# Mixture-of-experts kernel on one core: the second expert weight loaded after the row transposes, and scaled and split in its own expert's first stage

## Chip, cores and metric

The kernel runs on one core of a Trainium2 chip. The metric is the device time of one execution in microseconds; lower is better. The engines are named as in the profile: PE (TensorE, the matrix engine) with its weight loads PEld, DVE (VectorE), ACT (ScalarE), POOL (GpSimd) and SP (SyncE, which here only issues DMAs).

## The reference

Attention with a banded mask in half of the heads and a strided mask in the other half, and behind it a layer of experts with a capacity. Only the second part matters here:

```python
def _moe_ref(x, w_gate, w1, w2):            # x: 4608 tokens x 512
    N, D = x.shape                          # w1: 8 x 512 x 1024, w2: 8 x 1024 x 512
    E = w_gate.shape[1]                     # 8 experts
    cap = N // E                            # 576 tokens for each
    logits = x @ w_gate
    # all (token, expert) pairs in order of falling logit: a token goes to the
    # first expert that is not full, until every token has one
    ...
    for e in range(E):
        mask = assigned == e
        h = np.maximum(x[mask] @ w1[e], 0.0)
        out[mask] = h @ w2[e]
```

Since every expert takes exactly 576 tokens, the greedy assignment can be done expert by expert: the expert that fills first is closed, its tokens leave, and so on.

## The kernel before, in words

The attention part writes the tokens' rows to a scratch tensor in DRAM (`x_scr`) and the logits to SBUF. It ends before 205 us of the profiled execution. Behind it the eight experts follow one after the other, in an order that the data decide; the number `ph` counts them from 0 to 7.

**What is done for one expert.** A search with seven rounds (`search`, L809 to L861) finds the logit at which the expert is full. Each round compares all logits with 17 candidates on DVE (`cm`, L817), counts on PE (L833), adds up on DVE (`red` L836, `r` L839) and PE (L842), compares on DVE (`g`, L846 or L849), sums on PE (L852) and makes the next candidates on DVE (`cand`, L855). From the result come the expert's number (`ei`, L877), each token's slot (`slots`, L886 to L916) and the list of its rows (`indices`, L935 to L974, with two groups of matmuls on PE, L961 and L969). POOL gathers the rows (`xr`, L1078: five gathers of up to 128 rows), ACT and DVE cut each row into two f16 parts (`xg`, L1067 and L1068), and SP issues a DMA transpose for each (`xt`, L1069). The last expert needs no search (`rest`, L864).

**The weights** (`weights`, L976 to L1052). SP reads the expert's number into a register and issues the loads (L985): four of 512 KB for w1 and four of 512 KB for w2. Each weight has one f32 buffer, so a load waits until the expert before has no more use of it. For each weight there are then: four squares with a sum on ACT (`jk`, L1000), a scale (`ss` on DVE L1006, a matmul with ones on PE L1008, four small steps on DVE L204 to L209, which end in `w_sw`), and eight cuts (L1018 and L1019) in which ACT makes the upper f16 half (`w1h`, `w2h`) and DVE the lower one (`w1l`, `w2l`). The f16 halves have two buffers.

**The two stages of an expert on PE** (`ffn`, L1185). First stage: 8 blocks of 24 matmuls (`hidden`, L1175), each followed by the ReLU on ACT (`hh`, L1182) and its lower half on DVE (`hl`, L1183). Second stage: four and a half tiles of 128 rows, 24 matmuls each (L1223, the half one L1217); ACT scales the result (`y`, L1233), and POOL scatters it to the output (L1234). Before the second stage stand two small DVE steps, L1205 and L1206, that multiply the two weights' scales.

**What sets the order.** Only PE's order is written by hand: `ffn` yields the cost of each matmul to a clock, and generators (`chains`) that hold the side work have due times on that clock in ns. When one is due, its next step is emitted there, so that the PE instructions of the search, the indices and the scales stand at that place between the matmuls. In the first expert ACT's order is held too (`MANP`). For all the other engines what is emitted first has the higher priority, and what stands in `urgent()` a higher one still; a planner orders them by that when the whole program is known, and each engine then works through its queue in order.

For `ph` 1 and later the chain of the weights is one list: a step of 4000 ns (`T_W`), four squares of w1 (1500 ns each), its scale (1500), then four pairs of a cut of w1 and a square of w2, two more cuts of w1, the scale of w2, two cuts of w1 and eight cuts of w2 (1500 each). It starts when the expert's number is known, which is about when the first stage of the expert before ends. What is left of it when the own first stage begins is emitted at once (`rush`, in `spread`). For `ph` 0 there is a separate path (`start`, `more`, `later`), which the change leaves as it is.

The gather and the transposes are a chain of their own (`fetch`): the indices, then the five conversions and transposes in steps of 5000 and then 1200 ns, then 3000 ns more until the expert counts as ready.

Of the kernel before, what the change touches and what calls it, by code (L numbers as in the profile page):

```python
# [57 lines left out]
SCALE_AT, TURN_AT, TAKE_AT, SEARCH_AT, TURN_U, W_EARLY, TURNS, TURN_E = 7, 9, 9, 10, 0, 1, 3, 2  # L58
T_HOT6, T_CLOSE6 = 3200, 9000
T_F, T_LOAD0, T_HOT1, T_W, T_SQ, T_SCALE, T_CUT, T_BULK0 = 3000, 1500, 6350, 4000, 1500, 1500, 1500, 600  # L60
CUT0 = 1
# [76 lines left out]
def band_stride_attention_then_capacity_moe(ctx, tc, qt, kl, ks, nl, ns, wg, w1, w2, cst, out, dbg=None):  # L138
# [82 lines left out]
    with tc.tile_pool(name="ld", bufs=2) as ld, \  # L221
# [317 lines left out]
        todo = [Unit(b, strided) for b in range(B) for strided in (True, False)]  # L539
# [200 lines left out]
    def spread(ph, todo):  # L740
        for step, f in todo:
            if ph not in rush:
                yield step if ph else min(step, T_BULK0)
            f()

    def slowly(todo):
        for step, f in todo:
            yield min(step, T_STEP0) if step != T_W20 else step
            f()
# [226 lines left out]
    def weights(ph, ei):  # L976
        e = nc.sync.value_load(ei[0:1, 0:1], min_val=0, max_val=E - 1)
        res, todo = [], []
        for name, w, nch, width, bits in (("w1", w1, DC, FF, W1_BITS), ("w2", w2, FC, DM, W2_BITS)):
# [6 lines left out]

            k = W_EARLY if ph == 0 and name == "w2" else 4
            fetch_w(range(k))
            if k < 4:
                def later(wf=wf, k=k, n4=n4, go=fetch_w):  # L990
                    nc.gpsimd.memset(wf[:, k * n4:, :1], 0.0)
                    go(range(k, 4))
# [34 lines left out]
        if ph == 0:  # L1027
# [17 lines left out]
            return res, (start, more, later)  # L1045
        todo = [(T_W, lambda: None)] + sq1 + sc1
        for a, b in zip(cut1[:4], sq2):
            todo += [a, b]
        todo += cut1[4:6] + sc2 + cut1[6:] + cut2
        g = spread(ph, todo)  # L1050
        chains.append([due_now(), g])
        return res, g  # L1052

# [102 lines left out]
    def fetch(ph, slot, wts):  # L1156
        idx, sx = yield from indices(ph, slot)
        xt, todo = tokens(ph, idx)
        for t, f in enumerate(todo):
            yield T_ROWS if t == 0 else T_ROW  # L1160
            f()
        yield T_LOAD - T_ROWS
        work[ph] = wts[0], xt, idx, sx, wts[1]
        ready.add(ph)
# [20 lines left out]
    def ffn(ph, wts, xt, idx, sx):  # L1185
# [14 lines left out]
        else:  # L1200
            for f in range(FC):
                yield from hidden(wts, xt, hh, hl, f, (slice(0, HC), slice(HC, CAP)), ps_h.tile([128, 2, 512], F32, name="ph"))
        for _ in second[0] if ph == 0 else ():
            pass
# [3 lines left out]
        for t in (0, NT - 1, *range(1, NT - 1)):  # L1208
            tail = t == NT - 1
            py = ps_h.tile([128, 2, 512], F32, name="ph")[:, 0]  # L1210
            k = 0
# [49 lines left out]
    with tc.manual_schedule(engines=MAN):  # L1261
        work[0] = now[:4] + (now[4](),)
        chains.append([T_LOAD0, load0()])
        for ph in range(E):
            with tc.manual_schedule(engines=MAN0) if ph in MANP else nullcontext():
# [5 lines left out]
                for c in list(chains):  # L1271
                    if c[1] is work[ph][4]:
                        c[0] = clock
                        advance(c)
                for cost in ffn(ph, *work[ph][:4]):
                    clock += cost
# [70 lines left out]
```

## Time and profile before

| | |
|---|---|
| median of three runs | 678.89 us (674.91 to 679.88) |
| the profiled execution's own time | 676.12 us |
| its span, first to last instruction | 674.4 us |
| mean granted PE clock | 0.959 |
| w loads: number, size | 64 of 512 KB |
| HBM read / written | 73.60 MB / 18.87 MB |
| first stage of `ph` 0 begins | 220.36 us |
| second stage of `ph` 7 begins | 639.38 us |

A line of the timeline has the start in us, the duration in us (of the whole group, where equal instructions in a row are merged), the engine, the line of the kernel, the operation, output <- inputs by the program's names, the shape and the count. In brackets behind it stands how long the engine was idle before, and what released it. A group line has the busy time and the mean in ns of one instruction, then the idle time before the group. A line of the waits has: who waited for whom, us in total, times, the longest. Groups that overlap in the merged timeline share their place: a merged line shows the first start, and other instructions of that engine may stand inside it.

### The profile page before, as it was taken

The numbers are of one execution on the slowest core, as the hardware profiler recorded it, in microseconds if no ns is written. First come the engines' busy times: TensorE is split into PE (matmuls) and PEld (weight loads), VectorE is DVE, ScalarE is ACT, GpSimd is POOL, SyncE is SP. The second block draws the span as 40 slices with busy tenths as digits, with TensorE's granted clock in tenths as the row PEclk, the third lists the DMA queues.
The fourth block names the chain that finished last, engine by engine and source line by source line (L and its number), as shares of the span: only waits on it lengthen the run. The fifth ranks groups of instructions, "written<-read, shape, count | busy, mean of one in ns | idle before, by whom it ended". The sixth has DMA issues, their size and how long they took to land.

```text
span 674.4 us, 19427 instructions
## 1 busy us (share of the span) xinstructions
PE 602.9 (89%) x8125; PEld 394.4 (58%) x8128; DVE 456.9 (68%) x1381; ACT 333.0 (49%) x554; POOL 110.8 (16%) x124
## 2 busy tenths in 40 slices
PE   7789899999847788999899989989989997999993
PEld 4567676776633564476467458447646744746741
DVE  4858787788787787777686786777768648570200
ACT  2555554555303464843851871664384279761210
POOL 2101101111102000500420430240042041211011
PEclk9959999999967799999999999989999999899997
DMA  8888798887406406803921860860491197911010
GB/s 240 200 231 222 209 241 239 246 234 215 137 2 216 129 1 236 209 17 131 268 63 35 299 129 1 286 160 17 174 245 44 67 306 228 240 35 48 1 40 32
DMA packets 76363, 102.40 MB, mean 152 GB/s; under 512 B 41292, under 2 KB 49062, under 8 KB 75763
## 3 DMA queue, kind: packets, MB, share of 16 engines
q1 hardware_dynamic: 68195, 79.61, 41.5%
q0 software_dynamic: 7360, 21.15, 10.4%
q8 instruction: 64, 1.05, 0.6%
q10 hardware_dynamic: 720, 0.39, 0.2%
q14 instruction: 24, 0.20, 0.1%
HBM read 73.60 MB, written 18.87 MB: 137 GB/s over the span
## 4 chain that ended last, share of the span: by engine, by line
PE 46%; issue 16%; DVE 15%; DMA 11%; ACT 6%; POOL 3%; SPq 1%; another core or an unknown queue 0%; POOLq 0%; ACTq 0%; DVEq 0%
PE ph L1175 17%; PE ph L1223 7%; PE po L394 4%; PE spa L351 4%; DMA w<-in_w_dram 4%; DMA xr<-x_scr,idx 2%; DVE w2l L1019 2%; DVE w1l L1019 2%; POOL xr L1078 2%; ACT jk L292 2%; DMA v_s<-in_ns_dram 2%; POOL out_dram L1234 1%; PE spb L469 1%; PE spa L374 1%; ACT w1h L1018 1%
## 5 line engine op out<-in xcount | busy, mean ns | idle before, releaser
L1175 PE MATMUL ph<-xt,w1h 128*128 128x288 f16 (+2 forms) x1024 | 177.9, 289 | 7.0 <-DMA xt<-xg 4.5
L1175 PEld LDWEIGHTS <-w1h 128*128 128x128 f16 x1024 | 97.7, 99 | 38.0 <-issue 8.5
L1175 PE MATMUL ph<-xt,w1l 128*128 128x288 f16 (+2 forms) x512 | 111.8, 289 | 0.0
L1234 POOL DMA_INDIRECT out_dram<-y,idx x40 | 47.8, 1195 | 337.2 <-ACT y L1233 314.6
L1223 PE MATMUL ph<-w2h,hh 128*128 128x512 f16 x256 | 97.8, 382 | 0.0
L1223 PE MATMUL ph<-w2h,hl 128*128 128x512 f16 x256 | 97.7, 382 | 0.0
L1223 PE MATMUL ph<-w2l,hh 128*128 128x512 f16 x256 | 97.5, 381 | 0.0
L1182 ACT ACTIVATE hh<-ph 128x576 f16<-128x576 f32 (+2 forms) x72 | 42.8, 595 | 108.6 <-PE ph L1175 108.0
L1000 ACT ACTIVATE jk<-w 128x1024 f16<-128x1024 f32 x64 | 67.4, 1053 | 57.8 <-DMA w<-in_w_dram 56.8
L1223 PEld LDWEIGHTS <-hh 128*128 128x128 f16 x512 | 49.4, 98 | 57.4 <-issue 7.2
L1183 DVE SCALAR_TENSOR_TENSOR hl<-ph,hh 128x576 f16<-128x576 f32 (+2 forms) x72 | 49.5, 687 | 43.7 <-ACT hh L1182 43.5
L1175 PEld LDWEIGHTS <-w1l 128*128 128x128 f16 x512 | 50.4, 99 | 13.3 <-issue 0.6
L1078 POOL DMA_INDIRECT xr<-x_scr,idx x40 | 41.6, 1040 | 51.2 <-DMA w<-in_w_dram 25.3
L377 ACT ACTIVATE pr<-spa 128x576 f32<-128x576 f32 x32 | 20.8, 651 | 57.6 <-PE spa L374 52.7
L1223 PEld LDWEIGHTS <-hl 128*128 128x128 f16 x256 | 25.1, 98 | 39.6 <-issue 14.8
L1019 DVE SCALAR_TENSOR_TENSOR w1l<-w,w_sw,w1h 128x512 f16<-128x512 f32 x64 | 45.6, 742 | 3.7 <-ACT w1h L1018 2.5
L1019 DVE SCALAR_TENSOR_TENSOR w2l<-w,w_sw,w2h 128x512 f16<-128x512 f32 x64 | 46.3, 744 | 2.1 <-ACT w2h L1018 2.0
L1018 ACT ACTIVATE w2h<-w,w_sw 128x512 f16<-128x512 f32 x64 | 41.1, 710 | 6.6 <-DVE w_sw L209 6.6
L1018 ACT ACTIVATE w1h<-w,w_sw 128x512 f16<-128x512 f32 x64 | 42.8, 709 | 3.0 <-DVE ss_e L204 1.8
L1233 ACT ACTIVATE y<-ph,so 128x512 f32<-128x512 f32 x32 | 21.8, 680 | 44.5 <-PE ph L1223 30.7
L428 POOL DMA_DIRECT2D x_scr<-xs x23 | 16.5, 724 | 154.0 <-DVE vsum L297 101.4
L394 PE MATMUL po<-v_s,pr 64*54 64x65 f32 x768 | 31.3, 230 | 2.4 <-DMA v_s<-in_ns_dram 1.5
(619 smaller groups left out, 920.3 us busy)
## 6 DMA issues: line engine op xcount, KB each, us to landing
w<-in_w_dram SPq DMA_DIRECT2D x64, 512.0 KB
kl<-in_kl_dram SPq DMA_DIRECT2D x16, 304.0 KB
v_s<-in_ns_dram SPq DMA_DIRECT2D x16, 292.5 KB
v_l<-in_nl_dram SPq DMA_DIRECT2D x16, 292.5 KB
ks<-in_ks_dram SPq DMA_DIRECT2D x16, 288.0 KB
qs<-in_qt_dram SPq DMA_DIRECT2D x16, 288.0 KB
ql<-in_qt_dram SPq DMA_DIRECT2D x16, 288.0 KB
x_scr<-xl SPq DMA_DIRECT2D x8, 512.0 KB
```

Of the source, the lines that this page charges most:

```text
L351: nc.tensor.matmul(u.sp[p][64 * f:64 * f + m, h, o:o + n], u.kt[r, p * u.nk + c:p * u.nk + c + m], u.q[r, p, c:c + n], start=False, stop=F ...
L394: nc.tensor.matmul(po[r:r + u.nq, j - j0], pr[k, o:o + u.nq], u.vn[k, t, 2 * p + h], start=(j == j0), stop=(j == j1 - 1), skip_group_check ...
L1000: nc.scalar.activation(jk, wf[:, c * n4:(c + 1) * n4].rearrange("p c f -> p (c f)"), AF.Square, scale=1.41422, accum_out=sq[:, c:c + 1])
L1018: nc.scalar.activation(hi[:, c, f], wf[:, c, f], AF.Copy, scale=s_)
L1019: nc.vector.scalar_tensor_tensor(lo[:, c, f], wf[:, c, f], s_, hi[:, c, f], op0=OP.mult, op1=OP.subtract)
L1078: nc.gpsimd.indirect_dma_start(out=xr[:n], out_offset=None, in_=x_rows, in_offset=bass.IndirectOffsetOnAxis(ap=idx[:n, t:t + 1], axis=0))
L1175: nc.tensor.matmul(tile_[:, j, :w], wt[:, d, f * 128:(f + 1) * 128], xt[:, d // 2, xx, d % 2, c], start=(k == 0), stop=(k == 3 * DC - 1))
L1182: nc.scalar.activation(hv, src, AF.Relu)
L1183: nc.vector.scalar_tensor_tensor(lv, src, 0.0, hv, op0=OP.max, op1=OP.subtract)
L1223: nc.tensor.matmul(py, a[:, f, ts_], w[:, f], start=(k == 0), stop=(k == len(todo) - 1))
L1233: nc.scalar.activation(y, py, AF.Copy, scale=so[:, t:t + 1])
L1234: st = nc.gpsimd.indirect_dma_start(out=out_rows, out_offset=bass.IndirectOffsetOnAxis(ap=idx[:n, t:t + 1], axis=0), in_=y[:n], in_offset= ...
```

## The change

For `ph` 1 and later: the four loads of w2 are no longer issued in `weights` but by a function (`later`) that `fetch` calls after the last row conversion and transpose have been emitted. The chain of the weights ends with the eight cuts of w1, now 1500 ns apart without squares between them. The squares, the scale and the cuts of w2 form a chain of their own (`thirds`), which starts when the expert's own first stage starts: a step of 4000 ns, four squares and the scale 1500 ns apart, then the eight cuts 1000 ns apart. What is left of it is emitted at the end of the first stage. `ph` 0 is as before.

```diff
+T_W21, T_CUT2 = 4000, 1000
...
+    thirds = {}
+
+    def evenly(todo):
+        for step, f in todo:
+            yield step
+            f()
+
...
-            k = W_EARLY if ph == 0 and name == "w2" else 4
+            k = 4 if name == "w1" else 0 if ph else W_EARLY
             fetch_w(range(k))
-            if k < 4:
+            if k == 0:
+                later = lambda go=fetch_w: go(range(4))
+            elif k < 4:
                 def later(wf=wf, k=k, n4=n4, go=fetch_w):
                     nc.gpsimd.memset(wf[:, k * n4:, :1], 0.0)
                     go(range(k, 4))
...
-        todo = [(T_W, lambda: None)] + sq1 + sc1
-        for a, b in zip(cut1[:4], sq2):
-            todo += [a, b]
-        todo += cut1[4:6] + sc2 + cut1[6:] + cut2
-        g = spread(ph, todo)
+        g = spread(ph, [(T_W, lambda: None)] + sq1 + sc1 + cut1)
         chains.append([due_now(), g])
-        return res, g
+        thirds[ph] = evenly([(T_W21, lambda: None)] + sq2 + sc2 + [(T_CUT2, f) for _, f in cut2])
+        return res, g, later
...
         for t, f in enumerate(todo):
             yield T_ROWS if t == 0 else T_ROW
             f()
+        wts[2]()
         yield T_LOAD - T_ROWS
...
-        for _ in second[0] if ph == 0 else ():
+        for _ in second[0] if ph == 0 else thirds[ph]:
             pass
...
+                if ph:
+                    chains.append([clock, thirds[ph]])
                 for cost in ffn(ph, *work[ph][:4]):
```

## The prediction, on record before the changed kernel was run

> **What bounds the kernel now.** I read the page first, then TensorE (PE) in order of time for the stage boundaries, then the list of PE's waits, then ACT, DVE and SP around those waits.
>
> ```profile
> span 674.4 us, 19427 instructions
> PE 602.9 (89%) x8125; PEld 394.4 (58%) x8128; DVE 456.9 (68%) x1381; ACT 333.0 (49%) x554; POOL 110.8 (16%) x124
> ```
>
> PE is busy for 89% of the span, so a change beside PE can win only what PE loses in waits or at a lower clock. In order of time, the first matmul of each stage marks its start: L1175 opens a first stage, L1223 a second one.
>
> ```profile
> 422.38 0.38 PE L1223 MATMUL ph<-w2h,hh 128*128 128x512 f16 x1
> 453.50 0.65 PE L1175 MATMUL ph<-xt,w1h 128*128 128x288 f16 x4
> 479.07 0.38 PE L1223 MATMUL ph<-w2h,hh 128*128 128x512 f16 x1
> 560.14 0.28 PE L1175 MATMUL ph<-xt,w1h 128*128 128x288 f16 x1
> 592.09 0.38 PE L1223 MATMUL ph<-w2h,hh 128*128 128x512 f16 x1
> 615.86 0.65 PE L1175 MATMUL ph<-xt,w1h 128*128 128x288 f16 x4
> 639.38 0.38 PE L1223 MATMUL ph<-w2h,hh 128*128 128x512 f16 x1
> ```
>
> Number the experts 0 to 7 in order of work. Expert 3's second stage takes 453.50 - 422.38 = 31.1 us, expert 4's first stage 25.6 us, expert 6's first stage 32.0 us, and expert 7's, with no search beside it, 23.5 us. The first stages of the middle experts are near that floor; the second stages and expert 6's first stage are not. The waits of PE between 285 and 615 us say where (in total, times, longest):
>
> ```profile
> PE ph L1175 <- DMA xt<-xg: 4.5, 2, 2.9
> PE pr__7371 L842 <- DVE red L836: 2.5, 1, 2.5
> PE pr__9134 L961 <- DVE rv L947: 1.9, 1, 1.9
> PE pr__6686 L842 <- DVE r L839: 1.6, 1, 1.6
> PE pr__8136 L852 <- DVE g L849: 1.3, 1, 1.3
> PE pr__5841 L842 <- issue: 1.1, 1, 1.1
> PE pr__5841 L852 <- DVE g L849: 1.0, 1, 1.0
> PE pr__5921 L842 <- DVE r L839: 0.9, 1, 0.9
> PE pr__8216 L842 <- DVE r L839: 0.9, 1, 0.9
> ...
> PE pr__7560 L842 <- DVE r L839: 0.3, 1, 0.3
> ```
>
> Two waits are for transposed rows (xt), before experts 1 (1.6) and 6 (2.9). One is for expert 7's index tables (rv), inside expert 6's first stage. The seven after that, 9.3 us together, are steps of the threshold search (L842, L852) in the second stages of experts 1 to 4: PE's order is written by hand, a search matmul stands in it at a fixed place, and all matmuls behind it wait when DVE is late. The last row is the same wait in a first stage, where it is small. Twice PE also runs at a lower granted clock soon after a wait:
>
> ```profile
> 445.00:450.00 5.00, 5.00 (x18) 1.97 (x17) 4.82 (x10) 3.65 (x6) 1.71 (x1) 0.66 1.06 237
> 455.00:465.00 10.00, 9.71 (x94) 7.58 (x92) 9.43 (x24) 6.76 (x11) 0.61 (x1) 1.00 0.08 29
> 465.00:475.00 10.00, 10.00 (x100) 8.13 (x98) 5.62 (x16) 1.95 (x3) 0.00 (x0) 1.00 0.01 2
> 575.00:580.00 5.00, 5.00 (x39) 3.12 (x32) 1.23 (x4) 3.55 (x7) 2.09 (x3) 0.66 0.80 279
> ```
>
> Columns: stretch, its length, then busy us of PE, weight loads, DVE, ACT, POOL, the clock, DMA share, GB/s. 5 us at 0.66 cost 5 x 0.34 = 1.7 us each time.
>
> **Part 1: the load.** The change emits the second weight's four DMAs after the last row transpose instead of at once. Only PE keeps the emitted order here; the other engines, SP among them, are ordered by a planner. Does that order follow what is emitted, or what is ready?
>
> ```profile
> 422.64 5.08 SPq L985 DMA_DIRECT2D w<-in_w_dram  x8
> 441.50 7.77 SPq L1069 DMA_TRANSPOSE xt<-xg  x5
> ...
> 455.07 0.16 DVE L1205 TENSOR_TENSOR s<-w_sw,w_sw 128x1 f32<-128x1 f32 x1
> 538.07 0.13 DVE L877 TENSOR_SCALAR ei<-wm 1x1 int32<-1x1 f32 x1
> ...
> 433.41 1.06 ACT L1000 ACTIVATE jk<-w 128x1024 f16<-128x1024 f32 x1
> 437.55 1.93 ACT L1018 ACTIVATE w1h<-w,w_sw 128x512 f16<-128x512 f32 x3
> ```
>
> It follows what is ready. L1205 is emitted behind all matmuls of the first stage, which ends at 479.07, yet runs at 455.07, as soon as both scales exist: 24 us early. Expert 7's number (538.07) is emitted only once expert 5 is done (560.14): 22 us early. A square of the second weight (433.41) runs ahead of the first weight's cut (437.55), which is emitted before it. So I expect SP to do the same: between 427.7 (the eighth load issued) and 441.50 (the first transpose) SP has nothing ready, the expert's number is in its register, and the buffer is free, since the last cut of the expert before ends by then (Part 3). The four loads then go out directly behind the first weight's four, as now: **0 us**. The transposes keep their place in SP's queue. Should the loads really move, the gather and the transposes are passed by 2 MB less; that is the first rival.
>
> **Part 2: the squares.** Four squares per expert (1.05 us each) are now emitted in the expert's own first stage. They too become ready when the chunk lands and still fill ACT's gaps in the second stage before; but now they give way to every cut of the first weight, where before they stood between them.
>
> ```profile
> L1000 ACT ACTIVATE jk<-w 128x1024 f16<-128x1024 f32 x64 | 67.4, 1053 | 57.8 <-DMA w<-in_w_dram 56.8
> L1019 DVE SCALAR_TENSOR_TENSOR w2l<-w,w_sw,w2h 128x512 f16<-128x512 f32 x64 | 46.3, 744 | 2.1 <-ACT w2h L1018 2.0
> L1018 ACT ACTIVATE w2h<-w,w_sw 128x512 f16<-128x512 f32 x64 | 41.1, 710 | 6.6 <-DVE w_sw L209 6.6
> ```
>
> ```profile
> 389.12 1.04 ACT L1000 ACTIVATE jk<-w 128x1024 f16<-128x1024 f32 x1
> 394.34 0.73 DVE L1019 SCALAR_TENSOR_TENSOR w1l<-w,w_sw,w1h 128x512 f16<-128x512 f32 x1
> 395.24 0.17 PE L842 MATMUL pr__6686<-r,fold 68*128 68x8 f16 x1 [1.60 <-DVE r L839]
> ```
>
> One square stands at 389.12 between cuts; the cuts behind it come 1.04 us later on ACT, their DVE halves too (the last at 394.34), and the search's sum queues behind that half, so PE waits 1.60 us. The three waits of this kind are 1.6, 0.9 and 0.9. Each can shrink by at most the square: 1.0 + 0.9 + 0.9 = 2.8. A part of each is the half itself (0.73), which stays, so I take **-2.0**; bounds -3.4 (all three gone) and +1.0 (a square that fills a gap just ahead of a row conversion, once). The waits of 2.5, 1.3, 1.1 and 1.0 stand earlier, among the row conversions, and I leave them. Expert 1's 1.6 for xt and expert 6's 2.9 each have one square ahead of a row conversion (expert 6's at 550.67, below): at most 1.04 each; a cut can take the freed place, so **-0.5** each, bounds 0 and -1.04.
>
> **Part 3: scale and cuts.** The scale's matmul (L1008) moves from the stage's boundary to 11.5 us into it (4 + 4 x 1.5 + 1.5 by the planner's steps), the eight cuts behind it. What they cost on DVE is the same 8 x 0.744 = 5.95 us; today they also run in the own first stage, but at its head: from 455 to 465 DVE is busy for 9.43 of 10 us, from 465 to 475 for 5.62. Moved to 12 us, they need 5.95 us out of DVE's remaining share (1 - 0.56 = 0.44 of the time): 13.5 us at worst, 9 us as they run now, so done 21 to 25.5 us into a stage of 25.6. The second stage needs the eighth half only some 4.6 us after its start (23.8 us in expert 6 for four and a half tiles of eight groups: 5.3 a tile, seven eighths of it), so it is covered; without that cover each missing half would cost 0.74. The search steps that the cuts pass cost PE 0.3 us at the head of the stage (pr__7560); I expect the same at its tail, where that wait also holds the number of the next expert, which SP's loads are waiting for: **+0.2** for each of four experts, +0.8; bounds -1.2 (the 0.3 gone four times, none new) and the second rival. In the last expert all of it runs beside nothing: 0.
>
> In expert 6 it matters more:
>
> ```profile
> 550.67 1.04 ACT L1000 ACTIVATE jk<-w 128x1024 f16<-128x1024 f32 x1
> ...
> 564.46 3.40 DVE L1019 SCALAR_TENSOR_TENSOR w2l<-w,w_sw,w2h 128x512 f16<-128x512 f32 x5 [0.33 <-ACT w2h L1018]
> 573.14 0.66 DVE L947 TENSOR_TENSOR rv<-ohh,val 128x972 f16<-128x972 f16 x1
> ```
>
> DVE works on five halves at a stretch (and three more) before it builds rv for expert 7, and PE waits 1.9 us for rv. With the halves 12 us later, rv is some 5 us earlier: **-1.9**; bounds 0 and -1.9. The low clock at 575 follows this wait; if it goes with it, 1.7 us more. I take half: **-0.8**.
>
> The Trainium skill, "TensorE: Matmul & The Clock Gate", section "Why this matters for your kernels", says that the clock falls back after an idle gap of some 3 us. By that rule no wait of 1.9 us would cause the low clock at 575 and the term would be 0, the sum -4.1; here a low clock followed a wait of 1.9 and one of 2.5, which is why I keep half.
>
> **The sum:** -2.0 - 0.5 - 0.5 + 0.8 - 1.9 - 0.8 = -4.9 us. The profiled execution took 676.12 us (span 674.4 and 1.7 around it): 671.2. The median shown, 678.89, lies 2.8 above that execution; on its basis 678.89 - 4.9 = **674.0 us**, my forecast.
>
> **Rivals.** *The load and the squares really move.* For it: early starts are shown for DVE and ACT only, for no DMA of SP. Against it: those early starts. Then 4.2 us of squares leave ACT in each second stage and the gathers find the rings free: of the 9.3 us of search waits I count 60%, 5.6; both xt waits, 4.5; rv, 1.9; both low clocks in half, 1.7; less 0.8: 12.9, so 678.89 - 12.9 = 666.0.
>
> *Slower: the search starves at the tail.* Cuts, halves of the hidden layer and search share DVE between 12 and 25 us of each first stage of experts 1 to 5. If a late step there costs what a half in front of it costs in the second stages (mean of 1.6, 0.9, 0.9: 1.1), two rounds in five stages cost 11.0; with the 4.9 won elsewhere the time is 678.89 + 6.1 = 685.0. It decides from about 0.5 us per round on (5 us, which eats the gain). Against it: the same eight halves at the stage's head cost 0.3.
>
> *Nothing but the place changes.* The squares take their old gaps, the clock stays as it is, and only rv is won: 678.89 - 1.9 + 0.8 = 677.8.
>
> **How the numbers follow.** Forecast 0.45 (own range 670 to 678), the load moves 0.25, only the place changes 0.18, starved search 0.12. About 1% (6.8 us) is what a measurement of this kernel can tell from no change. Faster by more than that: most of the first rival (0.21) and a third of the forecast's own width (0.15), 0.36. Slower by more: half of the starved search and a little for orders not foreseen, 0.09. The rest, 0.55. From 661 (first rival with every search wait gone, 12.9 + 3.7 = 16.6, is 662) to 684 lies all but 0.15.
>
> **What would show it.** Right: eight loads in one run on SP ahead of the five transposes in experts 2 to 5; L1008 about 12 us into each own first stage and w2l from there to 21 to 25 us; no square between w1h cuts; no wait for rv; the waits of 2.5 to 1.0 in the second stages still there. Wrong: four loads behind the transposes (first rival), or L842 waits over 0.5 us in the last 13 us of a first stage (second). A first matmul of a second stage waiting for w2l would break Part 3.

## The result, and the profile after

The changed kernel is slower: 685.16 us median of 21 runs, beside 677.97 us for the kernel before, also 21 runs; ratio 1.0094, interval 1.0068 to 1.012. The forecast was 674.0, 4.9 us faster. Measured four more times, each in a series with other kernels, it gave 1.0002, 1.0087, 1.0066 and 1.0109: a part of the loss comes and goes. Where both parts lie is shown below; what brings the second one stays open.

The profiled execution after took 691.25 us, and its first expert stage begins at 228.62 us (220.36 before): 8.3 us lie in the attention part, which the change doesn't touch. That profile and those of the kernels `before3`, `first6b` and `sq_back` fell into a slower state of the chip; so the stages are compared, and a reading counts only where other profiles repeat it.

The order of time on PE, first matmul of each stage (L1231 opens a second stage, L1183 a first one): the second stages of experts 0 and 6.

```profile
264.32 0.38 PE L1231 MATMUL ph<-w2h,hh 128*128 128x512 f16 x1
...
298.41 0.78 PE L1183 MATMUL ph<-xt,w1h 128*128 128x288 f16 x4
...
604.66 0.38 PE L1231 MATMUL ph<-w2h,hh 128*128 128x512 f16 x1
...
630.96 0.29 PE L1183 MATMUL ph<-xt,w1h 128*128 128x288 f16 x1
```

Expert 0's second stage takes 34.1 us (29.5 before), expert 6's 26.3 us (615.86 - 592.09 = 23.8 before). All the other stages together are within 0.4 us of before. PE's waits from 285 to 640 us (in total, times, longest) name both:

```profile
PE pr__9101 L969 <- DVE rv L955: 3.9, 1, 3.9
PE pr__5070 L850 <- DVE r L847: 3.4, 1, 3.4
PE ph L1231 <- DVE w2l L1029: 2.1, 4, 0.6
...
PE ph L1183 <- DMA xt<-xg: 1.1, 2, 0.7
```

The wait for rv, forecast to go, is 3.9 instead of 1.9. The wait for w2l is new: it is the break of Part 3 that the prediction named, in expert 6. The wait of 3.4 for r is new in expert 0's second stage. The wait for xt shrank from 4.5 to 1.1.

Two things came as forecast. SP still issues eight loads in one run, ahead of the transposes; and ACT makes w1h without a square between (expert 4's, whose own scale matmul then stands at 478.58, 12.8 us into its first stage at 465.77):

```profile
436.21 4.98 SPq L993 DMA_DIRECT2D w<-in_w_dram  x8
455.11 8.10 SPq L1076 DMA_TRANSPOSE xt<-xg  x5
```

```profile
458.22 1.93 ACT L1028 ACTIVATE w1h<-w,w_sw 128x512 f16<-128x512 f32 x3
461.15 0.71 ACT L1028 ACTIVATE w1h<-w,w_sw 128x512 f16<-128x512 f32 x1
461.76 1.04 ACT L1010 ACTIVATE jk<-w 128x1024 f16<-128x1024 f32 x1
```

### Expert 6 in the profile after

ACT, DVE and the matmul of PE that waits for rv, in order of time, in expert 6's first stage (it begins at 573.05):

```profile
578.50 1.06 ACT L1010 ACTIVATE jk<-w 128x1024 f16<-128x1024 f32 x1 [4.42 <-DMA w<-in_w_dram]
...
582.35 0.63 ACT L1190 ACTIVATE hh<-ph 128x576 f16<-128x576 f32 x1
...
583.01 0.76 DVE L1191 SCALAR_TENSOR_TENSOR hl<-ph,hh 128x576 f16<-128x576 f32 x1 [8.42 <-ACT hh L1190]
...
586.23 0.66 DVE L955 TENSOR_TENSOR rv<-ohh,val 128x972 f16<-128x972 f16 x1
...
586.94 1.34 PE L969 MATMUL pr__9101<-ohl,rv 128*32 128x64 f16 x29 [3.94 <-DVE rv L955]
```

ACT works through its queue in order, and there the last expert's first square (578.50) now stands where expert 6's w2h cuts stood in the kernel before, whose first stage of expert 6 begins at 560.14:

```profile
563.70 3.17 ACT L1018 ACTIVATE w2h<-w,w_sw 128x512 f16<-128x512 f32 x5 [0.82 <-DVE w_sw L209]
```

The square's load has not landed: ACT idles 4.42 us, and the hh behind it, whose block PE ends at about 577, comes only at 582.35. DVE waits 8.42 for that hh, and rv, behind it on DVE, is late: it starts 13.2 us into the stage, and in the kernel before 13.0 (573.14 - 560.14). So rv is not the 5 us earlier that the forecast had; PE, which loses less at xt, only comes to it sooner. Later, and into the second stage:

```profile
593.22 0.17 PE L1018 MATMUL pr__9203<-ss,ones_b 128*128 128x1 bf16 x1
...
607.41 0.74 DVE L1029 SCALAR_TENSOR_TENSOR w2l<-w,w_sw,w2h 128x512 f16<-128x512 f32 x1
608.07 0.74 DVE L1029 SCALAR_TENSOR_TENSOR w1l<-w,w_sw,w1h 128x512 f16<-128x512 f32 x1
608.20 0.38 PE L1231 MATMUL ph<-w2l,hh 128*128 128x512 f16 x1 [0.57 <-DVE w2l L1029]
...
608.73 0.74 DVE L1029 SCALAR_TENSOR_TENSOR w2l<-w,w_sw,w2h 128x512 f16<-128x512 f32 x1
```

The scale of expert 6's second weight stands at 593.22, 20 us into the stage and not 11.5: in PE's hand-written order it follows the index matmuls, and they wait for rv. By then expert 7's first weight is ready to be cut too, and the two sets take turns on DVE. So w2l comes once in 1.32 us (608.73 - 607.41) while the second stage, begun at 604.66, wants one for each three matmuls of 0.22 (23.8 us for 108 in the kernel before): 0.66 us.

### The profile page after: what moved, and what is told of

Read it like the earlier page. It is cut to its first block, busy times and chain, and to the rows that moved or that the text cites. A ratio compares the mean times of both kernels' runs of the same rounds, so it can differ in the third digit from the quotient of the medians.

```text
span 689.5 us, 19424 instructions
## 1 busy us (share of the span) xinstructions
PE 613.8 (89%) x8125; PEld 399.8 (58%) x8128; DVE 454.7 (66%) x1381; ACT 333.0 (48%) x554; POOL 109.9 (16%) x124
## 4 chain that ended last, share of the span: by engine, by line
PE 41%; DVE 20%; issue 16%; DMA 10%; ACT 6%; POOL 3%; SPq 2%; another core or an unknown queue 0%; POOLq 0%; ACTq 0%; DVEq 0%
PE ph L1183 12%; PE ph L1231 6%; DMA w<-in_w_dram 5%; PE po L395 5%; PE spa L352 5%; DVE w2l L1029 3%; DVE w1l L1029 2%; DVE hl L1191 2%; PE spa L375 2%; DVE cm L825 2%; PE spb L470 1%; PE spb L453 1%; ACT jk L293 1%; ACT jk L1010 1%; POOL out_dram L1242 1%
## 5 line engine op out<-in xcount | busy, mean ns | idle before, releaser
L1183 PE MATMUL ph<-xt,w1h 128*128 128x288 f16 (+2 forms) x1024 | 177.7, 289 | 3.8 <-ACT xt L1067 2.1
L1183 PEld LDWEIGHTS <-w1h 128*128 128x128 f16 x1024 | 97.8, 98 | 32.9 <-issue 6.0
L1183 PE MATMUL ph<-xt,w1l 128*128 128x288 f16 (+2 forms) x512 | 112.2, 289 | 0.0
L1231 PE MATMUL ph<-w2l,hh 128*128 128x512 f16 x256 | 98.1, 383 | 2.1 <-DVE w2l L1029 2.1
L1231 PE MATMUL ph<-w2h,hl 128*128 128x512 f16 x256 | 98.3, 384 | 0.0
L1231 PE MATMUL ph<-w2h,hh 128*128 128x512 f16 x256 | 98.1, 383 | 0.0
L1231 PEld LDWEIGHTS <-hh 128*128 128x128 f16 x512 | 49.6, 99 | 61.7 <-issue 12.2
L1183 PEld LDWEIGHTS <-w1l 128*128 128x128 f16 x512 | 50.3, 98 | 15.5 <-issue 3.4
L1231 PEld LDWEIGHTS <-hl 128*128 128x128 f16 x256 | 25.1, 98 | 41.1 <-issue 17.0
L1075 DVE TENSOR_TENSOR xg<-xr,xg 128x512 f16<-128x512 f32 (+1 forms) x37 | 25.4, 688 | 15.1 <-ACT xg L1074 10.5
```

What stands on the lines that cost most here:

```text
L1075: nc.vector.tensor_tensor(xs[:, 1], xv, xs[:, 0], op=OP.subtract)
L1183: nc.tensor.matmul(tile_[:, j, :w], wt[:, d, f * 128:(f + 1) * 128], xt[:, d // 2, xx, d % 2, c], start=(k == 0), stop=(k == 3 * DC - 1))
L1231: nc.tensor.matmul(py, a[:, f, ts_], w[:, f], start=(k == 0), stop=(k == len(todo) - 1))
```

## The experiments

Theory A: the loss lies in experts 6 and 7, by the blocked ACT and the late w2l. Theory B: it lies in expert 0's second stage and the middle experts. The table has every kernel: ratio to the kernel before (with its 95% interval), then stage lengths of its profile in us, from the first matmuls as above: second stage of expert 0, experts 1 to 5 whole, first and second stage of expert 6. Chips are named A, B, C (for the first two rows it isn't recorded).

| kernel | chip | ratio | 0, second | 1 to 5 | 6, first | 6, second |
|---|---|---|---|---|---|---|
| before | | | 29.5 | 274.6 | 32.0 | 23.8 |
| after | | 1.0094 (1.0068 to 1.012) | 34.1 | 274.6 | 31.6 | 26.3 |
| `load_back` | A | 1.0006 (0.9966 to 1.0045) | 29.5 | 272.2 | 32.2 | 26.5 |
| `to5` | A | 0.9971 (0.9931 to 1.0012) | 28.9 | 271.6 | 32.2 | 23.8 |
| `only67` | A | 1.0061 (1.002 to 1.0102) | 28.2 | 272.7 | 32.7 | 26.1 |
| `late_load` | A | 1.0094 (1.0052 to 1.0136) | 28.4 | 276.5 | 32.2 | 26.5 |
| `again` (after) | A | 1.0002 (0.9966 to 1.0038) | 28.7 | 274.1 | 33.0 | 26.8 |
| `first6` | A | 0.9983 (0.9946 to 1.002) | 28.8 | 272.6 | 32.8 | 23.9 |
| `early6` | A | 1.0043 (1.0004 to 1.0082) | 29.0 | 271.0 | 37.1 | 23.5 |
| `sq_back` | A | 1.0009 (0.9962 to 1.0055) | 28.1 | 278.3 | 32.9 | 23.5 |
| `unblock` | B | 1.0114 (1.0053 to 1.0174) | 32.1 | 276.6 | 39.2 | 23.5 |
| `both` | B | 1.0127 (1.0091 to 1.0162) | 31.7 | 272.2 | 36.6 | 23.5 |
| `again2` (after) | B | 1.0087 (1.0055 to 1.0118) | 33.1 | 274.0 | 32.8 | 25.9 |
| `before2` (before) | C | 1.003 (0.9997 to 1.0064) | 28.1 | 273.1 | 31.8 | 23.8 |
| `from2` | C | 1.0058 (1.0026 to 1.0091) | 28.6 | 272.9 | 32.0 | 26.2 |
| `first6b` (`first6`) | C | 0.9994 (0.9953 to 1.0035) | 28.9 | 273.6 | 33.6 | 23.5 |
| `again3` (after) | C | 1.0066 (1.0024 to 1.0109) | 28.8 | 272.6 | 32.5 | 26.6 |
| `before3` (before) | B | 0.9991 (0.9943 to 1.0039) | 27.9 | 280.9 | 31.9 | 23.8 |
| `from2b` (`from2`) | B | 1.003 (0.9987 to 1.0074) | 27.8 | 277.7 | 31.6 | 26.6 |
| `again4` (after) | B | 1.0109 (1.0055 to 1.0163) | 32.7 | 273.7 | 32.9 | 25.1 |

Two columns speak at once. Expert 6's second stage is 23.8 us in each kernel with the old handling of expert 6 and 25.1 to 26.8 in each with the changed one unaltered. Expert 0's second stage is 27.8 to 29.5 us, save in five profiles: 31.7 to 34.1.

### Does the load matter, and does it move?

`load_back`: the four loads at their old place in the code.

```diff
-            k = 4 if name == "w1" else 0 if ph else W_EARLY
+            k = 4 if name == "w1" or ph else W_EARLY
...
-        return res, g, later
+        return res, g, (lambda: None)
```

> The changed kernel with one part undone: the four loads of the second weight are emitted in `weights` again, at once behind the first weight's four; the chains of squares, scale and cuts stay as changed. If the load's new place does nothing (the step of 0 us in the prediction), the time is that of the changed kernel, 1.009 of the kernel before (684 us), and the eight loads stand in one run on SP as there. If the load's new place costs the 6 us, it is 1.000 (678 us). Two theories on the loss, both of which this second look at the same order of work can weaken: A, it lies in experts 6 and 7 (ACT stands at a square of the last expert's weight whose load has not landed, then the halves of expert 6's second weight are late): the first stage of 6 plus its second stage are again 2 us longer than before and PE's wait for rv is again near 3.9. B, it lies in the second stage of expert 0, which took 34.1 us in the changed kernel's profile and 29.5 before: it is again near 34. If that was chance, it is near 29.5.

1.0006, where the changed kernel has 1.0002 on this chip (`again`, below). The order of work is the same as there on every engine, the loads on SP included, and no stretch of the table differs by more than 2 us. The step of 0 us for the load stands.

`late_load`: the load bound behind the last transpose on SP, so that it really moves.

```diff
-            nc.sync.dma_start_transpose(xt[:, :, t * 128:t * 128 + n], xg[:n])
+            turned.append(nc.sync.dma_start_transpose(xt[:, :, t * 128:t * 128 + n], xg[:n]))
...
+                    ld = nc.sync.dma_start(wf[:, c * n4:c * n4 + n4], src[:, c * n4:c * n4 + n4])
+                    if ph and name == "w2":
+                        tc.add_manual_dep(ld.ins, turned[-1].ins.name, mybir.DependencyInfo(
+                            mybir.DependencyClass.NoSync, mybir.DependencyReason.DATA), reason="behind the rows")
```

> The changed kernel with the second weight's four loads bound behind the last row transpose on SP's queue, for experts 1 to 7, so that the load really moves; squares, scale and cuts as changed. The first rival of the prediction (gathers and transposes find the rings free, 4.2 us of squares leave each second stage): 0.982 of the kernel before (666 us). Theory A: the blocked ACT in expert 6's first stage is untouched by this, so 1.004 to 1.010 (680 to 685 us) with the waits of the second stages smaller by a few us at most. Theory B: 1.004 to 1.010 as well, with the second stage of expert 0 near 34 us, if its stall does not hang on the second weight's squares; near 30 and 0.998 if it does.

1.0094, not 0.982: the first rival falls even where its condition is met. The second stages of experts 1 to 4 do get shorter, 115.4 us in sum against 118.2 in `load_back`. But the first stages of experts 1 to 5 take 135.8 us against 128.6. Expert 2's first stage (it begins at 344.05), ACT, DVE and PE in order of time:

```profile
346.12 1.06 ACT L1013 ACTIVATE jk<-w 128x1024 f16<-128x1024 f32 x1 [6.05 <-DMA w<-in_w_dram]
...
353.38 0.80 DVE L825 TENSOR_TENSOR cm<-rmn,cand 128x612 f16<-128x612 f32 x1
354.23 0.47 PE L841 MATMUL pr__6077<-ohn,cm 128*68 128x32 f16 x9 [1.58 <-DVE cm L825]
```

It is the picture of expert 6 again: ACT stands 6.05 us at a square whose load is under way, with hh behind it, and the search gets its cm late. The gain of the one stage is given back with interest in the next.

### Which experts carry the loss?

`to5` has the change for experts 1 to 5 only, `only67` for 6 and 7 only (`NEW` is the set of experts that get it; the others keep the old load and the old chain).

```diff
+NEW = (1, 2, 3, 4, 5)
...
-            k = 4 if name == "w1" else 0 if ph else W_EARLY
+            k = 4 if name == "w1" or ph and ph not in NEW else 0 if ph else W_EARLY
...
+        if ph not in NEW:
+            todo = [(T_W, lambda: None)] + sq1 + sc1
+            for a, b in zip(cut1[:4], sq2):
+                todo += [a, b]
+            todo += cut1[4:6] + sc2 + cut1[6:] + cut2
+            g = spread(ph, todo)
...
```

> The change for experts 1 to 5 only; experts 6 and 7 have the old load and the old chain. Theory A (the loss lies in experts 6 and 7): the loss is gone, 0.996 to 1.001 of the kernel before (675 to 679 us), the wait for rv is back at 1.9 and no second stage waits for w2l. Theory B (the loss lies in the second stage of expert 0 and the middle experts): 1.005 to 1.010 (681 to 685 us), with a second stage of expert 0 near 34 us.

> The change for experts 6 and 7 only; experts 1 to 5 have the old load and the old chain. Theory A: 1.005 to 1.010 (681 to 685 us): the wait for rv near 3.9, four waits for w2l of 0.5 in expert 6's second stage. Theory B: 1.000 to 1.003 (678 to 680 us), since the 2 us of expert 6 are all that is left and the second stage of expert 0 is near 29.5.

0.9971 and 1.0061, both as theory A had it, with expert 6's second stage at 23.8 and 26.1. On this chip theory B's stage was not long in any kernel (28.1 to 29.5), so these two runs can't speak on it. That `only67` comes out above the whole change (1.0002 and 1.0006) warns of the ratios: the intervals overlap, and the stage lengths are the sharper measure.

### What makes expert 6's second stage long?

`first6`: expert 6's eight cuts of w2 at the higher priority, so that they stand ahead of expert 7's w1 cuts. The scale's place is unchanged.

```diff
+        def ahead(f):
+            with urgent():
+                f()
+
...
-        thirds[ph] = evenly([(T_W21, lambda: None)] + sq2 + sc2 + [(T_CUT2, f) for _, f in cut2])
+        thirds[ph] = evenly([(T_W21, lambda: None)] + sq2 + sc2 + [
+            (T_CUT2, (lambda f=f: ahead(f)) if ph == E - 2 else f) for _, f in cut2])
```

> The changed kernel, with expert 6's eight cuts of the second weight given the higher priority, so that on ACT and DVE they stand ahead of expert 7's first-weight cuts instead of in turns with them; the scale keeps its place behind the index matmuls. Theory A (the late scale and the sharing of the cuts make w2l late): the wait for w2l falls from 2.1 to 0 to 0.5 and expert 6's second stage from 26.3 to 24.0 to 24.5 us; the wait for rv stays at 3.9. Rival (the scale alone, 20 us into the stage, is too late, whatever the order of the cuts): the wait stays at 1.5 or more and the stage over 25.5 us. Time: 2 us less than the changed kernel run beside it by A, the same by the rival.

DVE in the profile of `first6`, the cuts around the start of expert 6's second stage at 591.15:

```profile
587.69 2.74 DVE L1029 SCALAR_TENSOR_TENSOR w2l<-w,w_sw,w2h 128x512 f16<-128x512 f32 x4
591.02 2.07 DVE L1029 SCALAR_TENSOR_TENSOR w2l<-w,w_sw,w2h 128x512 f16<-128x512 f32 x3
593.67 0.74 DVE L1029 SCALAR_TENSOR_TENSOR w2l<-w,w_sw,w2h 128x512 f16<-128x512 f32 x1
594.33 1.41 DVE L1029 SCALAR_TENSOR_TENSOR w1l<-w,w_sw,w1h 128x512 f16<-128x512 f32 x2
```

No w1l between, no wait for w2l, the stage at 23.9 us. The first half comes 3.5 us before the stage begins, and in the changed kernel 3.2 (601.43), so it is the order that differs. The wait for rv is 3.9 as in the changed kernel. So the turns with expert 7's cuts are the cause, and the late scale alone is not. Repeated on another chip:

> first6 once more (expert 6's second-weight cuts ahead of expert 7's first-weight cuts), because its 0.9983 was measured where the changed kernel itself gave 1.0002. If the cuts' order is worth 2 to 2.5 us: again 0.003 to 0.004 below the changed kernel run beside it, expert 6's second stage at 23.8 to 24.0.

0.9994 there beside 1.0066 of the changed kernel, stage 23.5. The intervals overlap in both series, so the stage is the surer sign. `first6` takes the loss back; a version faster than the kernel before beyond the intervals did not come out of this study (the lowest is `to5`, 0.9971, up to 1.0012).

`early6`: expert 6's squares, scale and first cut of w2 due at once in its first stage.

```diff
+        at = 0 if ph == E - 2 else 1
-        thirds[ph] = evenly([(T_W21, lambda: None)] + sq2 + sc2 + [(T_CUT2, f) for _, f in cut2])
+        thirds[ph] = evenly([(T_W21 * at, lambda: None)] + [(t * at, f) for t, f in sq2 + sc2] + [(T_CUT2, f) for _, f in cut2])
```

> The changed kernel, with expert 6's squares, scale and first cut of the second weight due at the start of its first stage instead of 4 to 13 us later, so that the scale's matmul stands ahead of expert 7's index matmuls; experts 1 to 5 and 7 as changed. Theory A (expert 6 alone makes the loss; by its cuts ACT is also covered while the last expert's first weight is under way): wait for rv back to 1.8 to 2.0, no wait for w2l, expert 6's second stage 23.8 us, time as with the change in experts 1 to 5 alone, 0.995 to 1.000 of the kernel before. Rival (the loss is spread over the experts): 1.003 or more, with the second stage of expert 6 at 23.8 all the same.

A miss: the second stage is 23.5, but the wait for rv rose to 6.0 and the first stage to 37.1. The numbers of the rival came (1.0043, with that second stage), but not by its cause: experts 1 to 5 take 271.0 us, and the loss lies in expert 6's first stage. Its ACT, and PE at the index matmuls:

```profile
564.54 1.06 ACT L1010 ACTIVATE jk<-w 128x1024 f16<-128x1024 f32 x1 [4.82 <-DMA w<-in_w_dram]
...
567.21 1.93 ACT L1028 ACTIVATE w2h<-w,w_sw 128x512 f16<-128x512 f32 x3
...
577.09 1.50 PE L969 MATMUL pr__9128<-ohl,rv 128*32 128x64 f16 x36 [5.97 <-DVE rv L955]
```

The last expert's square still stands ahead of the w2h cuts, whose scale is made by then, and holds them and hh up. So the early scale takes the turns of the cuts away, and the wait for w2l with them, but it does not cover ACT against that square; there the order on ACT is what counts.

`unblock`: that square bound on ACT behind expert 6's hidden halves (`halved` lists them), and due 8 us later (`T_W7` is 12000). `both` is `unblock` with `first6`.

```diff
...
+                if ph == E - 1 and name == "w1":
+                    tc.add_manual_dep(a.ins, halved[-1].ins.name, mybir.DependencyInfo(
+                        mybir.DependencyClass.NoSync, mybir.DependencyReason.DATA), reason="behind the hidden layer")
...
+        g = spread(ph, [(T_W if ph < E - 1 else T_W7, lambda: None)] + sq1 + sc1 + cut1)
```

> The changed kernel, with the four squares of the last expert's first weight bound on ACT behind the halves of the hidden layer that expert 6's first stage has emitted by then (and due 12 us into that stage instead of 4), so that ACT no longer stands at a square whose load has not landed. Theory (the wait for rv has grown from 1.9 to 3.9 because that square holds ACT): the wait falls to 0 to 1.9, expert 6's first stage takes 29.5 to 31 us (31.6 to 33.0 in the changed kernel); the second weight's cuts then also run ahead of the last expert's first-weight cuts, so that expert 6's second stage takes 23.8 to 24.5 (26.1 to 26.8): 3 to 5 us less than the changed kernel run beside it, 0.993 to 0.998 of the kernel before. Rival (rv is late by its own DVE work, as before the change): the wait stays at 1.9 or more and the first stage over 31.6; only the second stage gains, 2.5 us.

> unblock and first6 together: the last expert's squares behind expert 6's hidden halves, and expert 6's second-weight cuts at the higher priority. If unblock already puts those cuts first, the same as unblock within 0.3%: first stage of expert 6 29.5 to 31 us, second 23.8 to 24.5. If the cuts at the higher priority get ahead of the row conversions of the last expert, or of the halves of the hidden layer, the wait for rv or for xt is longer by up to 1 us than in unblock.

PE's longest wait in `unblock`, from 562 to 602 us:

```profile
PE pr__9322 L1021 <- DVE ss L1019: 7.2, 1, 7.2
```

The wait for rv is gone, as the theory said, and rv starts 12.0 us into the stage in `unblock` and 9.9 in `both`, so the square did hold it; but both times are misses, 1.0114 and 1.0127. The square now comes so late that the scale matmul of the last expert's weight, fixed in PE's order, waits 7.2 us for its sum. Without that wait the stage would be 39.2 - 7.2 = 32.0 us in `unblock` and 36.6 - 6.8 = 29.8 in `both`: whether the wait for rv costs anything net stays open.

### What are the squares worth in experts 1 to 5?

`sq_back`: squares among the w1 cuts and the load as before the change; scale and cuts of w2 as changed.

```diff
-        g = spread(ph, [(T_W, lambda: None)] + sq1 + sc1 + cut1)
+        todo = [(T_W, lambda: None)] + sq1 + sc1
+        for a, b in zip(cut1[:4], sq2):
+            todo += [a, b]
+        g = spread(ph, todo + cut1[4:])
...
-        thirds[ph] = evenly([(T_W21, lambda: None)] + sq2 + sc2 + [(T_CUT2, f) for _, f in cut2])
+        thirds[ph] = evenly([(T_W21 + 4 * T_SQ, lambda: None)] + sc2 + [(T_CUT2, f) for _, f in cut2])
...
```

> The changed kernel with the load in its old place and the four squares of the second weight again between the first weight's cuts, as before the change; the second weight's scale and cuts keep their new place. The term of -2.0 in the prediction said that squares among the cuts cost the search waits 2 us over the second stages of experts 1 to 5. If so, these five stages are 2 us longer in sum than in the changed kernel (to5: 147.2 us for the second stages of experts 1 to 5 without the sixth's, load_back 143.6 for experts 1 to 5), and waits of 1.6 and two of 0.9 for r are back; if the squares' place costs nothing, the sum is the same within 0.7 us. Expert 6 as in the changed kernel (26.3) by both.

(The 147.2 in that text is a slip: in `to5` the five stages sum to 143.1.) The second stages of experts 1 to 5 sum to 147.3 us against 143.6 in `load_back`, but 3.6 of that are expert 2's alone (33.0 us); the other four sum to 114.3, and to 114.1 in `load_back`. The waits for r are back at 3.0, 2.1, 1.6 and 1.6. And expert 6 is a miss: 23.5, not 26.3, with the scale as late as in the changed kernel (21.1 us into the stage); there the w2 cuts mostly got ahead of expert 7's, and five halves are begun before the second stage, against three in the changed kernel. Where the waits for r go shows in PE's waits from 300 to 535 us, the kernel before (`before2`) and the changed one (`again3`), same chip:

```profile
PE pr__8216 L842 <- DVE r L839: 2.3, 1, 2.3
PE pr__6686 L842 <- DVE r L839: 1.9, 1, 1.9
PE pr__5921 L842 <- DVE r L839: 1.6, 1, 1.6
PE pr__7451 L842 <- DVE r L839: 1.6, 1, 1.6
...
PE pr__5921 L833 <- DVE cm L817: 0.8, 1, 0.8
```

```profile
PE pr__7447 L850 <- DVE r L847: 1.4, 1, 1.4
PE pr__8212 L841 <- DVE cm L825: 1.1, 1, 1.1
PE pr__7447 L841 <- DVE cm L825: 1.0, 1, 1.0
PE pr__5917 L850 <- DVE r L847: 0.9, 1, 0.9
PE pr__6682 L850 <- DVE r L847: 0.9, 1, 0.9
PE pr__8212 L850 <- DVE r L847: 0.9, 1, 0.9
...
PE pr__6682 L841 <- DVE cm L825: 0.7, 1, 0.7
...
PE pr__5917 L841 <- DVE cm L825: 0.5, 1, 0.5
```

The four waits for r fall from 7.4 to 4.1, and waits for cm in the same search rounds rise from 0.8 to 3.3: of the 3.3 us won at r, PE keeps 0.8. The first profile of the kernel before is not like `before2`: its waits of this kind are 3.4 in sum, beside 3.2 in after.

### Why 1.0002 here and 1.0109 there?

The changed kernel unaltered, four times:

> The changed kernel once more, unaltered. load_back has the same order of work on every engine and gave 1.0006 of the kernel before (interval 0.9966 to 1.0045) where the changed kernel had given 1.0094 (1.0068 to 1.012). If the 6 us belong to the kernel, 1.007 to 1.012 again; if most of them lay in that first measurement, 1.000 to 1.005, and the loss that belongs to the change is the 2.5 us of expert 6's second stage less about 1 us won in experts 1 to 5: 1.002. By the stages: second stage of expert 6 at 26.1 to 26.5 us (23.8 before), second stage of expert 0 at 28 to 30 (34.1 was chance), wait for rv 3.9.

> The changed kernel a third time, unaltered. The first measurement gave 1.0094 (1.0068 to 1.012), the second 1.0002 (0.9966 to 1.0038), and load_back with the same order of work 1.0006. If the first is the kernel's own, 1.007 or more; if the stages tell the truth (second stage of expert 6 longer by 2.5 to 3 us, about 1 us won in the search waits of experts 1 to 5), 1.000 to 1.004.

> The changed kernel, unaltered, beside the three others. It gave 1.0094, 1.0002 and 1.0087. If the second stage of expert 0 decides between the two values: 1.007 to 1.010 with that stage at 31.5 us or more, 0.999 to 1.003 with it at 28 to 30.

> The changed kernel beside these two. With the stop in the second stage of expert 0 (31.5 us or more): 1.007 to 1.010 of the kernel before. Without it (28 to 30): 1.001 to 1.006, the 2.5 to 3 us of expert 6's second stage less what the search waits give.

On chip B expert 0's second stage is 33.1 and 32.7 us and the ratio 1.0087 and 1.0109; on A and C it is 28.7 and 28.8 and the ratio 1.0002 and 1.0066. (The 1.0066 lies above the 0.999 to 1.003 expected there; the stage that was to decide does not decide alone.) The place of the difference, in `again2` on chip B (DVE, POOL and PE):

```profile
279.82 0.68 DVE L1075 TENSOR_TENSOR xg<-xr,xg 128x512 f16<-128x512 f32 x1
...
280.99 1.01 POOL L1242 DMA_INDIRECT out_dram<-y,idx  x1 [0.30 <-issue]
...
283.05 0.18 DVE L844 TENSOR_TENSOR red<-pr__5070,fold 68x32 f16<-68x32 f32 x1 [2.55 <-remote]
...
284.07 0.17 PE L850 MATMUL pr__5070<-r,fold 68*128 68x8 f16 x1 [3.37 <-DVE r L847]
```

and in `again` on chip A:

```profile
275.44 0.18 DVE L844 TENSOR_TENSOR red<-pr__5070,fold 68x32 f16<-68x32 f32 x1
...
276.02 3.21 POOL L1242 DMA_INDIRECT out_dram<-y,idx  x1 [0.30 <-ACT xg L1074]
```

It is the same instruction in the same order. On chip B DVE stops 2.55 us in front of red, with its input from PE done, and POOL's scatter takes 1.01; on chip A DVE goes on and the scatter takes 3.21 (spans on POOL are rough), which nobody waits for. Behind the stop PE waits 3.4 us for r, and 0.7 to 0.8 in the profiles of the same order without it; in three of the five profiles with the stop a lower clock follows (start, length, busy us of PE, weight loads, DVE, ACT and POOL, the clock, DMA share, GB/s; this is after):

```profile
284.30:289.30 5.00, 1.78 (x6) 0.67 (x6) 2.79 (x8) 2.01 (x4) 1.01 (x1) 0.74 0.73 148
289.30:294.30 5.00, 5.00 (x16) 1.86 (x15) 1.93 (x6) 1.83 (x4) 0.87 (x1) 0.58 0.55 104
```

In `unblock` and `both` the clock stays at 1.00 behind the same stop, and the stage takes 32.1 and 31.7 us.

Is it the changed order or the chip? `from2` and `from2b` have the change for experts 2 to 7 only, so that the second stage of expert 0 is as before (`NEW = (2, 3, 4, 5, 6, 7)`); `before2` and `before3` are the kernel before.

> The kernel before, unaltered, as a yardstick: its ratio to itself shows what an interval of this measurement is worth (1.000, within 0.004, if the intervals hold), and its profile gives a second look at the second stages: 28.0 to 31.1 us for experts 0 to 4, 25.4 and 23.8 for 5 and 6, and whether DVE's unexplained stop of 1.7 us ahead of a red of the search (expert 3 in the first profile) comes at the same instruction again (if it hangs on the order of work) or not (if it is chance).

> The change for experts 2 to 7 only; expert 1, whose loads and halves fall into the second stage of expert 0, is as before. Theory D: the changed order in that stage makes DVE stop for 2.6 us at a red of the search, and that costs 3.5 to 4.5 us where it happens (second stage of expert 0: 34.1, 33.1, 32.1, 31.7 in four profiles; 28.4 to 29.5 in the others of the same order). Then here that stage takes 28 to 30 us, no stop there, and the time is 3 us or more below the changed kernel run beside it if that shows the stop, equal to it if not. Rival: the stop hangs on the chip and the moment, not on the order, and comes here too (31.5 us or more) where the changed kernel beside it has it.

> The kernel before, unaltered, for its profile. Theory D (the changed order of work in the second stage of expert 0 brings DVE's stop of 2.6 us): that stage takes 28 to 30 us here, whatever the changed kernel beside it shows. Rival (the stop hangs on the chip): 31.5 us or more if the changed kernel beside it has it. Ratio to itself 1.000, within 0.004.

> The change for experts 2 to 7 only, once more. Theory D: second stage of expert 0 at 28 to 30 us and no stop of DVE in it, even if the changed kernel beside it has the stop; expert 6's second stage 26.1 to 26.8. Rival (chip): 31.5 us or more together with the changed kernel.

Chip B again, first the changed kernel (`again4`), then the kernel before (`before3`):

```profile
258.19 0.38 PE L1231 MATMUL ph<-w2h,hh 128*128 128x512 f16 x1
...
290.92 0.28 PE L1183 MATMUL ph<-xt,w1h 128*128 128x288 f16 x1
```

```profile
261.81 0.38 PE L1223 MATMUL ph<-w2h,hh 128*128 128x512 f16 x1
...
289.76 0.28 PE L1175 MATMUL ph<-xt,w1h 128*128 128x288 f16 x1
```

32.7 against 27.9 us, and 27.8 in `from2b`, whose ratio is 1.003 beside 1.0109. On chip C neither `before2` (28.1) nor `from2` (28.6) nor the changed kernel has the stop. So, by these profiles, it takes both: the changed order in that stage, and that chip; every profile with both has the stop (four on chip B), and none with one alone has it there. It rests on the stages: the ratio of `from2b` and that of `again4` beside it have intervals that overlap. And stops of the kind are not bound to that stage: `from2b` has two in the second stages of experts 1 and 2, 4.4 us together, and the first profile of before one of 1.67 in expert 3's, which `before2` and `before3` don't have. `before2` against itself gave 1.003, so differences of 0.3% are not read from one series.

What the stop is stays open. Either of POOL's scatter and DVE may hold up the other, or a third thing both; that was not tried apart. The times don't show the scatter coming first: in `again2` DVE is done with xg at 280.50 (279.82 + 0.68) and could begin red, and the record of the scatter begins at 280.99; the same 0.5 us lie between the two in after, `unblock` and `both`, and only in `again4` does the scatter begin earlier. The Trainium skill, "SBUF — State Buffer", section "SBUF: two separate sides", says that DVE and GpSimd share one pair of ports, which the first to come holds alone while the other stands still; for DVE it names instructions in a two-port mode, and, against a GpSimd instruction that reads SBUF, those with two inputs in SBUF. Here red takes one of its two inputs (pr) from where PE writes its results, so it isn't shown that it falls under this; no run here shows that it is this lock.

## Why the prediction was wrong

- **Load, 0 us:** right. SP kept its order, and in `load_back` the place in the code changes neither the order nor the time beyond the interval.
- **Squares, -2.0:** mis-sized. Experts 1 to 5 took 273.2 us on the mean of the twelve profiles with the change there (271.0 to 276.6), and 273.5 on that of before, `before2` and `only67`: -0.2, less than their scatter. (`before3` has 280.9, which no other profile without the change repeats.) The waits for r shrank as argued from `before2` to `again3` (7.4 to 4.1), but waits for cm took most of it. The bounds held; the inner step "Each can shrink by at most the square" left out that the next search step is late as well.
- **xt, -0.5 twice:** the waits shrank, in sum from 4.5, 2.5 and 5.4 (before, `before2`, `before3`) to 1.0 to 2.5 in the five profiles of the changed kernel.
- **Scale and cuts in the middle experts, +0.8:** right in kind. In expert 4's stage the scale stands at 12.8 us and the last half begins at 22.3 (21 to 25 forecast), no second stage of experts 1 to 5 waits for w2l, and the first stages have one wait of 0.4 for r each (0.3 before). The starved search did not come, save in `late_load`, by another way.
- **rv, -1.9, and the clock, -0.8:** the step that failed first. The prediction saw that DVE would be free of the halves, and not that the same halves' upper parts kept ACT at work; in their place ACT stands at the last expert's square. So rv, forecast some 5 us earlier, starts 13.2 to 14.1 us into the stage in the five profiles of the changed kernel, and 13.0, 13.4 and 14.4 in the three of the kernel before. With the change in experts 6 and 7 unaltered the wait is 3.7 to 3.9 us (5.1 in `late_load`) and the low clock stayed (0.66 from 586 to 591 us in after). The kernel before itself has 1.9, 4.2 and 1.3 in its three profiles, so the 1.9 was one draw of several. Net it moved little: expert 6's first stage is 32.36 us on the mean of the ten profiles with the change there unaltered and 31.95 on the mean of the four without (before, `before2`, `before3`, `to5`), +0.4, as the wait for xt shrank.
- **"The second stage needs the eighth half only 4.6 us after its start, so it is covered":** broken in expert 6. The 11.5 us were 20, and eight halves of the next weight came between. The stage went from 23.8 to 26.3 us on the mean of ten, **+2.5**. In after PE waits four times for a half, 0.5 us each and not the 0.74 that the prediction put on a missing one. `first6` shows the cause.
- **Expert 0's second stage, put at nothing:** +3.9 on the mean (32.9 in `again2` and `again4` against 29.0 in `load_back`, `again`, `again3`), on one chip. The prediction had no term for a stop of DVE; what brings it stays open.

The sum that the stages give is -0.2 + 0.4 + 2.5 = +2.7 us (1.004), and +6.6 (1.010) with the stop. Measured: 1.0006, 1.0002 and 1.0066 without it; 1.0094, 1.0087 and 1.0109 with it.

## What to carry to other kernels

Work that is moved away from an in-order engine leaves a place, and what moves up there may be an instruction that waits for a transfer, as the square at which ACT idled 4.42 us: look for the next instruction in the queue that isn't ready, and count what stands behind it. A cover must be checked in the stage that differs from the others (here expert 6, with index work on PE and the next weight's cuts beside it), not in the mean one. Where the work of two stages becomes ready at once, say which goes first; the priority of eight cuts was worth 2.5 us.

## Not expected of the hardware

The same order of work is as fast as the kernel before on one chip (1.0002) and 1.1% slower on another (1.0109), with one stop of DVE of 1.7 to 2.6 us in the second case, which came at this place only with that order of instructions around it. And the same wait of PE, 3.4 us behind that stop, was followed by a clock of 0.58 to 0.66 in three profiles (after, `again2`, `again4`) and of 1.00 in two (`unblock`, `both`). The Trainium skill, "TensorE: Matmul & The Clock Gate", section "Why this matters for your kernels", puts the gap that lowers the clock at some 3 us: 3.4 lies close to such a border, but in the kernel before the clock was 0.66 soon after waits of 1.9 and 2.5, which that rule does not give.
